# Chunk attention and a routed expert layer: v loaded by pairs of chunks over all 128 partitions, in a ring of eight places

## The chip, the cores and the metric

The kernel runs on one core of a Trainium2 chip. The metric is the device time of one execution, in microseconds (us). Three timed runs of the kernel before gave 680.16, 674.33 and 673.17 us; their median is 674.33 us. One further execution was recorded by the hardware profiler, and all views below come from it.

## The reference

Two blocks follow each other. The first is attention inside chunks of 64 rows: for each of 8 batches and 8 heads, 576 rows of 64 numbers are cut into 9 chunks, and a row sees only its own chunk.

```python
scores = scale * np.matmul(q_c, k_c.transpose(0, 1, 2, 4, 3))
scores = scores - np.max(scores, axis=-1, keepdims=True)
attn = np.exp(scores)
attn = attn / (np.sum(attn, axis=-1, keepdims=True) + 1e-09)
out = np.matmul(attn, v_c)
```

The result becomes 4608 tokens of 512 numbers. The second block sends each token to the one of 8 experts whose embedding is most alike (cosine), computes `relu(x @ w1[e]) @ w2[e]` with w1 of 512 x 1024 and w2 of 1024 x 512, and scales by the probability of that expert. All is float32: q, k and v are 9.4 MB each, w1 and w2 16.8 MB each.

## The kernel before, in words

**Tiles of the attention.** A pair of chunks is 128 rows, so the 72 chunks of all batches make NT = 36 pairs, counted by t. A pair may cross from one batch to the next. For each pair q and k of all 8 heads are loaded as [128 rows, 8 heads, 64] (`load_qk`). `turn_qk` transposes them on TensorE. `scores` makes, for each of 4 head pairs i, each parity of the head (par) and each of the pair's two chunks (c), one 64x64x64 matmul. Its operands lie in rows 64*par and up of SBUF, its result in rows 64*c and up of one of two PSUM banks, the bank of par. VectorE subtracts the maximum, ScalarE takes the exponential (`weights`), TensorE transposes back (`turn_a`), and `values` multiplies with v, which carries a column of ones that gives the row sum. `values` ends with VectorE writing x into `xr`, a ring of NX = 8 places, and GpSimd (POOL) writing the row numbers beside it (the iota of L681).

**v before.** `load_v(b)` (L592 to L601) loads a whole batch: for each head one transfer into 64 partitions (even heads partitions 0 to 63, odd heads 64 to 127), 9 chunks of 256 bytes in each partition. Two buffers `v0` and `v1` alternate by batch. Batch 0 comes in two parts (chunks 0 to 3, then 4 to 8), batch 1 at t = 1, and each later one when pair t nears it; a buffer must have been read to its last chunk before its next batch may be loaded.

**The order of the work.** Everything is recorded in the order in which the code is written (L1037 to L1094): a loop over t from -3 to 38 issues `turn_a(t)`, `turn_qk(t+3)`, `load_qk(t+7)`, `scores(t+2)`, `turn_x(t-1)`, `values(t)`, `weights(t+2)`, and, every fourth pair, the routing (`logits`, `pick`, `place`). Each engine and each DMA queue works through its own list in that order and stops at the first item whose inputs aren't there. Two queues matter. SP's queue holds the first four k tiles, all of v, nine transfers that clear places of the table `spots` (`clear_first`, L567 and L569), then the first expert inputs (`load_early` at t = 26 to 28 and 33) and the first expert weights (`load_first`, w1 at t = 28, w2 at t = 30). GpSimd's queue holds q, the other k tiles, the iota, small constants (one group in each round to t = 16), and `put`: an indirect transfer (L813) that scatters the finished x rows of a pair to `spots` by expert. The x of pair w is put in round w + 6, and its place in `xr` is wanted again by pair w + 8. In the built program a transfer on a queue also waits until the one eight before it has landed.

**The experts.** From `hidden_part` on, groups of 64 tokens for two experts at a time go through w1 (`hidden_fast`, a seven-product scheme, L328) and w2 (`result`, L401), about 37 steps. w1 for the first steps is used from t = 34 on (`early_parts`). `result` ends with ScalarE scaling into a tile `y` of one buffer (L420, L421) and an indirect transfer of it to the output (L428). For this input the last step is an odd one with one group of tokens (`one_group`, 256 columns).

Of the kernel before, what the change touches and what calls it, by code (L numbers as in the profile page):

```python
# [9 lines left out]
FP32 = mybir.dt.float32  # L10
# [8 lines left out]
P = 128  # L19
CH = 64  # L20
# [5 lines left out]
def kernel(  # L26
# [11 lines left out]
    nc = tc.nc  # L38
    B, H, S, Dh = q.shape
    E, D = moe_expert_emb.shape  # L40
    F = moe_w1.shape[2]
    N = B * S
    NPAIR = H // 2
    KD = D // P
# [4 lines left out]
    Q = 32  # L49
# [355 lines left out]
    def result(j, ps_y):  # L405
        d = mo.pop(j)
        ps = ps_y.tile([P, D], FP32, tag="y", name="y_ps")
        one_group = j == LEAST
        w = D // 2 if one_group else D
        for c in range(KF):  # L410
            for r in range(P // Q):
                t0, s, d0 = (r % 2, 0, w * (r // 2)) if one_group else (r, r // 2, 0)
                nc.tensor.matmul(  # L413
                    ps[Q * r : Q * r + Q, 0:w],
                    lhsT=d["hT"][:, c, Q * t0 : Q * t0 + Q],
                    rhs=w2_sb[s][buf_of(j)][:, c, d0 : d0 + w],
                    start=(c == 0),
                    stop=(c == KF - 1),
                )
        y = bp.tile([P, D], FP32, tag="y", name="y", bufs=1)  # L420
        nc.scalar.activation(y[:, 0:w], ps[:, 0:w], AF.Copy, scale=gate_of.pop(j))  # L421
        to, at, bound = out, spot[:, j % SPOTS, TOK : TOK + 1].bitcast(I32), N - 1
        if one_group:

            at2 = bp.tile([P, 1], I32, tag="at2", name="at2")
            nc.vector.tensor_scalar(at2, at, 2.0, second, ALU.mult, ALU.add)
            to, at, bound = out.rearrange("n (s d) -> (n s) d", s=2), at2, 2 * N - 1
        ins = nc.gpsimd.indirect_dma_start(  # L428
            out=to,
            out_offset=bass.IndirectOffsetOnAxis(ap=at, axis=0),  # L430
            in_=y[:, 0:w],
            in_offset=None,
            bounds_check=bound,
            oob_is_err=False,
        )
        tc.declare_no_dep(ins.ins, group="rows", reason="blocks hold different tokens")
        tc.add_to_no_dep_group("rows", ins.ins)
# [8 lines left out]
    with (  # L446
# [7 lines left out]
    ):  # L454

        pad(one, 40, "pad_one")
        v_sb = [one.tile([P, NPAIR, NCB, VW], FP32, name=f"v{i}") for i in range(2)]
        NX = 2 * RB
        xr = one.tile([P, NX, W], FP32, name="xr")
        blank = one.tile([P, W], FP32, name="blank")  # L460
# [108 lines left out]
            nc.sync.dma_start(out=spots[SPARE : SPARE + G, :], in_=blank[0:G])  # L569

        before = one.tile([P, E], BF16, name="before")
        qk_t, qkT, v_t, st = {}, {}, {}, {}

        def load_qk(t):

# [13 lines left out]
                    done += n  # L589
                qk_t[nm, t] = x.rearrange("p h d -> p (h d)")  # L590

        def load_v(b, c0=0, c1=NCB, eng=nc.sync):  # L592

            t = v_sb[b % 2]
            for h in range(H):
                r0 = CH * (h % 2)
                eng.dma_start(
                    out=t[r0 : r0 + CH, h // 2, c0:c1, 0:Dh],
                    in_=v[b, h].rearrange("(c k) d -> k c d", k=CH)[:, c0:c1],
                )  # L600
            v_t[b] = t  # L601

        def turn_qk(t):
            for nm in ("kx", "qx"):
# [11 lines left out]
        def scores(t):  # L616
            qx, kx = qkT.pop(("qx", t)), qkT.pop(("kx", t))
            ps = ps_s.tile([P, 2, 512], FP32, tag="sc", name="sc")
            sc = ps[:, :, 0 : NPAIR * CH].rearrange("p r (i k) -> p r i k", k=CH)
            for i in range(NPAIR):  # L620
                for par in range(2):
                    for c in range(2):
                        r0, c0 = CH * par, CH * c
                        nc.tensor.matmul(
                            sc[CH * c : CH * c + CH, par, i],
                            lhsT=qx[r0 : r0 + CH, i, c0 : c0 + CH],
                            rhs=kx[r0 : r0 + CH, i, c0 : c0 + CH],
                            start=True,
                            stop=True,
                        )  # L630
            mx = wk.tile([P, 2, NPAIR], FP32, tag="mx", name="mx")
            nc.vector.tensor_reduce(mx, sc, axis=AX.X, op=ALU.max)
            a = wk.tile([P, NPAIR, 2, CH], FP32, tag="a", name="a", bufs=3)
            nc.vector.tensor_tensor(
                a.rearrange("p i r k -> p r i k"),
                sc,
                mx.unsqueeze(3).to_broadcast([P, 2, NPAIR, CH]),
                ALU.subtract,
            )
            st[t] = {"a": a}  # L640
# [14 lines left out]
        def values(t):  # L655
            d = st[t]
            ps = ps_v.tile([P, 2, 512], FP32, tag="pv", name="pv")
            pv = ps[:, :, 0 : NPAIR * (Dh + 1)].rearrange("p r (i d) -> p r i d", d=Dh + 1)
            for i in range(NPAIR):
                for par in range(2):  # L660
                    for c in range(2):
                        b, cb = divmod(2 * t + c, NCB)
                        r0 = CH * par
                        nc.tensor.matmul(
                            pv[CH * c : CH * c + CH, par, i],
                            lhsT=d["aT"][r0 : r0 + CH, i, CH * c : CH * c + CH],
                            rhs=v_t[b][r0 : r0 + CH, i, cb, 0 : Dh + 1],
                            start=True,
                            stop=True,
                        )  # L670
            rs = wk.tile([P, 2, NPAIR], FP32, tag="rs", name="rs")
            nc.vector.tensor_scalar(rs, pv[:, :, :, Dh], 1e-9, None, ALU.add)
            nc.vector.reciprocal(rs, rs)
            x = xr[:, t % NX, 0:D]
            nc.vector.tensor_tensor(
                x.rearrange("p (i r d) -> p r i d", r=2, d=Dh),
                pv[:, :, :, 0:Dh],
                rs.unsqueeze(3).to_broadcast([P, 2, NPAIR, Dh]),
                ALU.mult,
            )  # L680
            nc.gpsimd.iota(  # L681
                xr[:, t % NX, D + TOK : D + TOK + 1].bitcast(I32),
                pattern=[[0, 1]],
                base=P * t,
                channel_multiplier=1,
            )
            st[t] = {"x": x}
# [318 lines left out]
        load_qk(1)  # L1006
        for x in v_sb:
            nc.vector.memset(x[:, :, :, Dh : Dh + 1], 1.0)
        load_v(0, 0, 4)
        load_qk(2)  # L1010
        load_qk(3)
        norm_experts()
        nc.gpsimd.memset(xr[:, :, D:W], 0.0)
# [18 lines left out]
                hidden_part(j, s, b, w1_sb, None, None, ps)  # L1032

        early_t = 26
        ends = {sum(sizes[: b + 1]) - 1: b for b in range(len(sizes))}
        constants, clears = constant_parts(), clear_first()
        for t in range(-3, NT + 3):  # L1037

            if 0 <= t < NT:
                turn_a(t)  # L1040
            if t == early_t - 1:
                count_early()
            if t + 3 < NT:
                turn_qk(t + 3)
                if t + 7 < NT:
                    load_qk(t + 7)
            if t == -2:
                load_v(0, 4, NCB)
            if t - 2 in ends:
                logits(ends[t - 2])  # L1050
            if t == NT:
                turn_x(t - 1)
            early_parts(t, 0)
            if 0 <= t + 2 < NT:
                scores(t + 2)
            if t - 2 in ends:
                copy_logits(ends[t - 2])
            if 0 <= t - 1 < NT - 1:
                turn_x(t - 1)
            if t - 3 in ends:  # L1060
                place(ends[t - 3])
            if 0 <= t < NT:
                values(t)
                b = (2 * t + 2) // NCB + 1
                if b not in v_t and b < B and t > 1:
                    load_v(b)
            if t == NT - 8:
                load_first(w1_sb, w1_rows)
            if t == NT - 6:
                load_first([w[0] for w in w2_sb], w2_rows)  # L1070
            if 0 <= t + 2 < NT:
                weights(t + 2)
            if t - 2 in ends:
                pick(ends[t - 2])
            if early_t <= t < early_t + XBUF:
                load_early(t - early_t)

            put(1 if t < NT - 2 else 2)
            if t == NT - 3:
                turn_xb(0)  # L1080
                load_early(XBUF)
            if t == NT - 1:
                turn_xb(1)
            early_parts(t, 1)
            if t == -2:
                turn_experts()
            if t >= 0:
                next(constants, None)
            if t >= 1:
                next(clears, None)  # L1090
                next(clears, None)
            if t == 1:
                load_v(1)
        groups()  # L1094
        pad_places()
        put(len(to_put))
# [148 lines left out]
```

## Time and profile before

| | |
|---|---|
| median of 3 runs | 674.33 us (673.17 to 680.16) |
| profiled execution, its own time | 673.4 us |
| its span (first to last record) | 671.6 us |
| TensorE (PE) busy over the span | 626.3 us, 93% |
| VectorE (DVE), ScalarE (ACT), GpSimd (POOL) busy | 425.9, 427.7 and 175.2 us |
| first and last `values` of the attention | start at 20.80 and 160.91 us |
| q1 (SP's queue): packets, bytes | 82824, 72.84 MB |
| q0 (GpSimd's queue): packets, bytes | 11696, 38.04 MB |
| transfers of v | 72, all from SP, 64 to 144 KB each |

How to read it: a line of the page or of the timeline gives the engine, the line of the kernel (L664 is line 664), the operation, output and inputs, and shape. In the timeline the first two numbers are start and length in us; like instructions in a row are merged, so a merged length covers their overlap. A bracket at the end tells how long the engine had been idle just before, and whose end released it. SPq is the issuing of transfers on SP, not their landing. The DMA row is the mean busy share of the core's 16 DMA engines; overlapping packets can make a share above 1.

### The profile page before, as it was taken

Reading aid. Unit: us, or ns where it says so; the run is one execution under the profiler, and the core shown is the slowest. Engines: PE = TensorE matmul, PEld = TensorE weight load, DVE = VectorE, ACT = ScalarE, POOL = GpSimd, SP = SyncE. Lnnn points to the kernel's source line nnn. Section 1 sums busy time; section 2 is a strip of 40 time slices with the busy share of each in tenths; the row PEclk is TensorE's granted clock in tenths of the full one; section 3 lists DMA queues with packets and bytes.
Section 4 is the critical chain, followed back from the end, with each engine's and each line's share of the span. In section 5 each row is a group of like instructions: output and inputs, shape, how many; then the busy total and the mean of one; then the engine's idle time right before and its main releaser. Section 6 shows DMA issues by size and latency. Waiting matters only on the chain. (4 is left out here: it accounts for less than half of the span.)

```text
span 671.6 us, 24878 instructions
## 1 busy us (share of the span) xinstructions
PE 626.3 (93%) x9744; PEld 343.6 (51%) x9744; DVE 425.9 (63%) x1140; ACT 427.7 (64%) x758; POOL 175.2 (26%) x255
## 2 busy tenths in 40 slices
PE   4988999999899979999999999988999999999993
PEld 3867888786343436555434444433444444444441
DVE  2858888886498535656576566768565667565430
ACT  4656677675225837674867877565877766867740
POOL 6648887843320101002110102202101020100101
PEclk9889899999899979999999999999999999999998
DMA  9898899989818711112787111776821114511101
GB/s 246 221 267 232 245 290 289 278 247 367 316 45 300 294 34 46 44 39 61 286 313 254 54 36 47 283 283 227 325 77 37 50 44 164 175 43 34 50 26 39
DMA packets 94687, 112.67 MB, mean 168 GB/s; under 512 B 52460, under 2 KB 72684, under 8 KB 94552
## 3 DMA queue, kind: packets, MB, share of 16 engines
q1 hardware_dynamic: 82824, 72.84, 34.0%
q0 software_dynamic: 11696, 38.04, 17.1%
q8 instruction: 81, 1.33, 0.8%
q14 instruction: 54, 0.44, 0.2%
q10 hardware_dynamic: 32, 0.02, 0.0%
HBM read 334.71 MB, written 22.69 MB: 532 GB/s over the span
## 5 line engine op out<-in xcount | busy, mean ns | idle before, releaser
L413 PE MATMUL y_ps<-w,hT 128*32 128x512 f32 (+1 forms) x2368 | 265.4, 591 | 3.6 <-DMA w<-in_moe_w_dram 3.6
L361 ACT ACTIVATE h<-C 64x256 f32<-64x256 f32 x264 | 179.0, 678 | 101.8 <-DVE C L374 99.4
L413 PEld LDWEIGHTS y_ps<-w,hT 128*32 128x32 f32 x2368 | 84.1, 111 | 160.0 <-issue 147.6
L428 POOL DMA_INDIRECT out_dram<-y,spot x36 | 35.1, 975 | 414.9 <-ACT y L421 238.7
L374 DVE TENSOR_TENSOR C<-C,h 128x256 f32<-128x256 f32 x231 | 96.1, 416 | 49.8 <-DVEq L299 39.2
L342 PE MATMUL h<-sums,xbT 128*32 128x256 f32 x1056 | 81.0, 380 | 5.0 <-DVEq L299 2.6
L342 PE MATMUL h<-w,S 128*32 128x256 f32 x1056 | 81.4, 379 | 3.2 <-DVE w L291 1.7
L342 PE MATMUL h<-w,xbT 128*32 128x256 f32 x1056 | 68.5, 379 | 0.0
L368 DVE STREAM_TRANSPOSE hT<-h 128x512 f32<-128x512 f32 x66 | 46.7, 708 | 28.2 <-ACT h L361 28.1
L227 DVE TENSOR_SCALAR rn<-rn 128x1 f32<-128x1 f32 x37 | 5.7, 153 | 82.3 <-ACT rn L224 82.3
L342 PEld LDWEIGHTS h<-w,xbT 128*32 128x32 f32 x1056 | 37.7, 110 | 34.1 <-issue 17.0
L342 PEld LDWEIGHTS h<-sums,xbT 128*32 128x32 f32 x1056 | 38.5, 110 | 28.8 <-ACT C L377 4.3
L342 PEld LDWEIGHTS h<-w,S 128*32 128x32 f32 x1056 | 39.1, 110 | 26.0 <-DVE C L374 2.0
L421 ACT ACTIVATE y<-y_ps,gate 128x512 f32<-128x512 f32 (+1 forms) x37 | 25.2, 682 | 37.5 <-issue 25.9
L813 POOL DMA_INDIRECT spots<-xr,dest x36 | 37.4, 1038 | 30.3 <-DVE dest L778 9.8
L203 DVE STREAM_TRANSPOSE xbT<-xin 128x256 f32<-128x256 f32 x73 | 44.5, 649 | 0.5 <-DVE hT L368 0.5
L224 ACT ACT_TABLE_LOAD x34 | 43.6, 1283 | 0.9 <-issue 0.4
L231 ACT ACT_TABLE_LOAD x34 | 43.6, 1283 | 0.6
L342 PE MATMUL h<-sums,S 128*32 128x256 f32 x528 | 40.9, 379 | 0.0
L695 ACT COPY xT<-tr 128x512 f32<-128x512 f32 x36 | 21.1, 585 | 29.9 <-PE tr L693 29.9
L585 POOL DMA_DIRECT2D kx<-in_k_dram x36 | 32.0, 891 | 19.1 <-PE tr L608 18.3
L585 POOL DMA_DIRECT2D qx<-in_q_dram x40 | 34.5, 866 | 0.3 <-PE tr L608 0.2
(202 smaller groups left out, 801.6 us busy)
## 6 DMA issues: line engine op xcount, KB each, us to landing
w<-in_moe_w_dram SPq DMA_DIRECT2D x74, 2048.0 KB
next_w<-in_moe_w_dram SPq DMA_DIRECT2D x67, 2048.0 KB
xin<-spots SPq DMA_DIRECT2D x158, 64.0 KB
qx<-in_q_dram POOLq DMA_DIRECT2D x32, 256.0 KB
v<-in_v_dram SPq DMA_DIRECT2D x56, 144.0 KB
kx<-in_k_dram POOLq DMA_DIRECT2D x28, 256.0 KB
spots<-blank SPq DMA_DIRECT2D x9, 144.0 KB
spot<-spots SPq DMA_DIRECT2D x80, 4.0 KB
```

The source lines that it names most:

```text
L203: nc.vector.transpose(xT[:, :, cols].rearrange("p c (b i) -> p b c i", i=Q), t[:, s * (D // 2) : (s + 1) * (D // 2)].rearrange("p (b i c) ...
L224: nc.scalar.activation(rn, spot[:, j % SPOTS, SQ : SQ + 1], AF.Sqrt)
L231: nc.scalar.activation(sh, sh, AF.Exp, accum_out=gate)
L342: nc.tensor.matmul(ps[t0 : t0 + Q], lhsT=a[:, c, s], rhs=w[:, r], start=c == 0, stop=c == KD // 2 - 1,)
L361: nc.scalar.activation(h[b][G * v : G * v + G, s].rearrange("p (k i) -> p k i", i=Q), x[G * s : G * s + G].rearrange("p (i k) -> p k i", i=Q),
L368: nc.vector.transpose(hT.rearrange("p k (s b i) -> p b s k i", b=2, i=Q)[:, b], h[b].rearrange("p s (k i) -> p s k i", i=Q),)
L374: nc.vector.tensor_tensor(out, a, b, op)
L413: nc.tensor.matmul(ps[Q * r : Q * r + Q, 0:w], lhsT=d["hT"][:, c, Q * t0 : Q * t0 + Q], rhs=w2_sb[s][buf_of(j)][:, c, d0 : d0 + w], start= ...
L421: nc.scalar.activation(y[:, 0:w], ps[:, 0:w], AF.Copy, scale=gate_of.pop(j))
L428: ins = nc.gpsimd.indirect_dma_start(out=to, out_offset=bass.IndirectOffsetOnAxis(ap=at, axis=0), in_=y[:, 0:w], in_offset=None, bounds_ch ...
L585: eng.dma_start(out=x[done : done + n], in_=src[b, :, s : s + n, :].rearrange("h p d -> p h d"),)
L813: ins = nc.gpsimd.indirect_dma_start(out=spots, out_offset=bass.IndirectOffsetOnAxis(ap=at, axis=0), in_=m, in_offset=None, bounds_check=S ...
```

## The change

Three things change.

- v is loaded by windows of two chunks: `load_v(w)` makes one transfer of 128 partitions x 4 heads x 64 for the even heads and one for the odd heads. Even heads hold chunks 2w and 2w+1; odd heads are shifted by a chunk and hold 2w-1 and 2w. At a batch's border a transfer is split in two. The window lies in place w % 8 of a ring of NV = 8.
- So that each operand lies in the right rows, `scores` writes (par, c) to bank `par ^ c`, and `values` takes rows `64 * (par ^ c)` and window t + par*c; the bank of its result stays par.
- Window t + 5 is issued in round t (29 and 30 in round 24, 31 and 32 in round 25), from SP; windows 33 to 36 go through GpSimd's queue in rounds 26 to 29, ahead of `turn_qk` and `load_qk`. Windows 0 and 1 stand between the first k tiles.
- Apart from v, the last odd step writes its result into a tile of the tag `S` and no longer into `y`.

```diff
-        y = bp.tile([P, D], FP32, tag="y", name="y", bufs=1)
+        if one_group:
+            S = late_p.tile([P, 3, KD // 2, 2, Q], FP32, tag="S", name="S", bufs=2)
+            y = S.rearrange("p a c b i -> p (a c b i)")
+        else:
+            y = bp.tile([P, D], FP32, tag="y", name="y", bufs=1)
...
-        v_sb = [one.tile([P, NPAIR, NCB, VW], FP32, name=f"v{i}") for i in range(2)]
+        NV = 8
+        v_sb = [one.tile([P, NV, NPAIR, VW], FP32, name=f"v{i}") for i in range(2)]
...
-        def load_v(b, c0=0, c1=NCB, eng=nc.sync):
-            t = v_sb[b % 2]
-            for h in range(H):
-                r0 = CH * (h % 2)
-                eng.dma_start(
-                    out=t[r0 : r0 + CH, h // 2, c0:c1, 0:Dh],
-                    in_=v[b, h].rearrange("(c k) d -> k c d", k=CH)[:, c0:c1],
-                )
-            v_t[b] = t
+        def load_v(w, eng=nc.sync):
+            for r in range(2):
+                c0, c1 = max(2 * w - r, 0), min(2 * w - r + 2, 2 * NT)
+                while c0 < c1:
+                    b, cb = divmod(c0, NCB)
+                    n = min(c1 - c0, NCB - cb)
+                    p0 = CH * (c0 + r - 2 * w)
+                    eng.dma_start(
+                        out=v_sb[r][p0 : p0 + CH * n, w % NV, :, 0:Dh],
+                        in_=v[b, r::2, CH * cb : CH * (cb + n), :].rearrange("h p d -> p h d"),
+                    )
+                    c0 += n
...
-                            sc[CH * c : CH * c + CH, par, i],
+                            sc[CH * c : CH * c + CH, par ^ c, i],
...
-                        b, cb = divmod(2 * t + c, NCB)
-                        r0 = CH * par
+                        r0 = CH * (par ^ c)
...
-                            rhs=v_t[b][r0 : r0 + CH, i, cb, 0 : Dh + 1],
+                            rhs=v_sb[par][r0 : r0 + CH, (t + par * c) % NV, i, 0 : Dh + 1],
...
-        load_v(0, 0, 4)
+        load_v(0)
         load_qk(2)
+        load_v(1)
         load_qk(3)
...
+        ahead_v = {t: [t + 5] if t < 24 else [] for t in range(-3, NT + 3)}
+        ahead_v[24], ahead_v[25] = [29, 30], [31, 32]
+        for i in range(4):
+            ahead_v[early_t + i] = [33 + i]
...
+            for w in ahead_v[t]:
+                load_v(w, nc.sync if t < early_t else nc.gpsimd)
...
-            if t == -2:
-                load_v(0, 4, NCB)
...
-                b = (2 * t + 2) // NCB + 1
-                if b not in v_t and b < B and t > 1:
-                    load_v(b)
...
-            if t == 1:
-                load_v(1)
```

More of the change, by code (lines that the diff above doesn't have):

```diff
@@ L571 @@
         before = one.tile([P, E], BF16, name="before")
-        qk_t, qkT, v_t, st = {}, {}, {}, {}
+        qk_t, qkT, st = {}, {}, {}
         def load_qk(t):
```

## The prediction

> **What bounds the kernel now.** I began with the page's busy rows and slices.
>
> ```profile
> PE 626.3 (93%) x9744; PEld 343.6 (51%) x9744; DVE 425.9 (63%) x1140; ACT 427.7 (64%) x758; POOL 175.2 (26%) x255
> PE   4988999999899979999999999988999999999993
> DMA  9898899989818711112787111776821114511101
> ```
>
> TensorE is the bound over most of the span. The exceptions are the first slices (16.8 us each) and the end of the attention, where the DMA row is at 8 or 9 and POOL is busy too. The change touches only that first quarter and the last few us, so I then took SP's and TensorE's timelines there.
>
> ```profile
> 1.87 5.62 SPq L597 DMA_DIRECT2D v<-in_v_dram  x8
> 7.54 2.10 SPq L585 DMA_DIRECT2D kx<-in_k_dram  x2
> 9.68 7.49 SPq L597 DMA_DIRECT2D v<-in_v_dram  x8
> 22.36 1.19 SPq L567 DMA_DIRECT2D spots<-blank  x2
> 23.59 9.02 SPq L597 DMA_DIRECT2D v<-in_v_dram  x8
> ```
>
> ```profile
> 14.36 1.09 PE L608 MATMUL tr<-ident,kx 128*128 128x128 f32 x4 [3.89 <-DMA kx<-in_k_dram]
> ...
> 34.13 1.02 PE L664 MATMUL pv<-v,aT 64*64 64x65 f32 x22
> 36.45 0.33 PE L664 MATMUL pv<-v,aT 64*64 64x65 f32 x4 [1.29 <-DMA v<-in_v_dram]
> 37.69 1.07 PE L664 MATMUL pv<-v,aT 64*64 64x65 f32 x6 [0.91 <-DMA v<-in_v_dram]
> 43.63 0.69 PE L664 MATMUL pv<-v,aT 64*64 64x65 f32 x32
> ```
>
> Two holes belong to v. The third k tile stands behind eight v transfers on SP, is issued at 7.54, and TensorE idles 3.89 us for it at 14.36. Batch 1 stands behind the clears, which wait for a GpSimd memset; it is issued from 23.59 to 32.6, and pair 4 needs it at 34.13. From pair 4 to pair 5 takes 43.63 - 34.13 = 9.5 us.
>
> An undisturbed round lasts 3.3 us from one `values` to the next, and 4.1 to 4.4 where routing falls in. Four rounds took 15.2 us at best with q and k loads running (43.63 to 58.82, 76.66 to 91.90), 3.8 us each. The 35 rounds took 160.91 - 20.80 = 140.1; 35 x 3.8 = 133 and the pair 4 hole (9.5 - 4.3 = 5.2) make 138, so about 2 us are left, nearly all between 58.8 and 76.7 (17.8 us for four). There DVE and POOL show why:
>
> ```profile
> 66.02 0.69 DVE L675 TENSOR_TENSOR xr<-pv,rs 128x512 f32<-128x512 f32 x1 [0.90 <-DMA spots<-xr,dest]
> ```
>
> ```profile
> 133.06 1.05 POOL L813 DMA_INDIRECT spots<-xr,dest  x1 [0.18 <-POOL xr L681]
> ...
> 140.03 0.12 POOL L681 IOTA xr<- 128x1 int32 x1 [2.75 <-DMA spots<-xr,dest]
> ```
>
> A place in `xr` is reused eight pairs on, and its put is issued in the second round before that, some 7 us earlier. The put of 133.06 belongs to the place that the iota of 140.03 wants, so it had taken some 6 us to land. That is close to the limit.
>
> The end:
>
> ```profile
> 657.55 0.69 ACT L421 ACTIVATE y<-y_ps,gate 128x512 f32<-128x512 f32 x1 [5.62 <-issue]
> ...
> 661.68 0.47 ACT L421 ACTIVATE y<-y_ps,gate 128x256 f32<-128x256 f32 x1 [3.45 <-DMA out_dram<-y,spot]
> 662.43 0.99 POOL L428 DMA_INDIRECT out_dram<-y,at  x1 [2.95 <-ACTq L1199]
> ```
>
> The last y waits until the y before it has left its only buffer; TensorE's merged line ends at 650.36 + 10.50 = 660.86.
>
> [...] put waits occur while SP sends v (54.8 to 66). [...] Before, each row half kept to its own bank; after, each half writes both. The trace doesn't show such a case.
>
> **The change, part by part.** Durations are of the profiled execution, span 671.6 us.
>
> 1. *First k tiles.* SP now issues two v transfers, not eight, ahead of the third k: at about 0.65 us each (median of the 72) k goes out near 3 us. Ahead of it on SP are 0.70 MB, and GpSimd's q takes an equal share; 2 x 0.96 MB at the 227 GB/s of the first 10 us are there after 8.5 us, so by 9 to 10. TensorE would want it at 14.36 - 3.89 = 10.47. The fourth k stands one window further: 1.47 MB on SP, about 3 MB in all, near 13, wanted at 18.20 - 3.89 = 14.3. I take the whole hole: -3.9; with q slowed a little, at least -2.5.
>
> 2. *Pair 4.* Windows 0 to 7 wait for no reader, so they follow the k tiles at once; window 5, which pair 4 needs, is the twelfth and thirteenth of the first 17 v transfers. SP's 3.0 MB and GpSimd's equal share end near 25 us, window 5 earlier; pair 4 comes at 34.13 - 3.9 = 30.2. The hole goes: -5.2. What is late next is q and k, on half the rate: tile 7 has about 3.1 MB of GpSimd's queue to itself and ahead, lands near 25, and is wanted near 27.5. Loss up to 1.
>
> 3. *Steady rounds.* The transfers are about as many (72, now 80: 36 even and 37 odd windows and seven splits) and have the same runs and bytes, so SP's issue costs nothing while nothing else waits on SP. A round moves q 0.26, k 0.26, v 0.26 and the put 0.29 MB: 1.08 MB in 3.8 us is 284 GB/s. The slices of before reached 304 to 316 (60 to 70, 80 to 90 and 100 to 110 us). v comes evenly instead of 1.15 MB at a time, so the put waits near 60 to 76 should shrink: -1.5. Bounds: -3.5 (all that is above 3.8 a round) to +4 (each of some 20 rounds 0.2 late).
>
> 4. *GpSimd's queue, rounds 26 to 29.* Seven transfers at the 0.9 us of a k or q issue are 6.3 us. A round there has k 0.92, q 0.90, iota 0.16 and put 1.05, 3.0 us; with v 4.8, against 3.8. So GpSimd falls back by about 1 us a round, 3 us by round 28. Behind v stand q and k (wanted four rounds on, covered), and the puts, which have no such cover: those of rounds 27 and 28 land 2 to 3 us later, and VectorE's write to `xr`, then TensorE's transpose, wait. The put of 133.06 was already late for the iota by 2.75, which cost TensorE little, as VectorE came to that `xr` only later. I take +1.5, bounds 0 and +5. SP meanwhile is free of batch 7 (issued until 134) and starts w1 earlier than 146; nothing on TensorE waited for w1 or w2 at 157 to 182, so this is worth nothing.
>
> 5. *`par ^ c`.* Number and order of the matmuls stay, and so do two column tiles in a bank at once. 32 pieces (16 matmuls, two each) take 0.6 us. I take 0: in each column half the two row halves still write different banks. Bounds: -0.05 a block (2 blocks x 36, -3.6) [...].
>
> 6. *End.* y of the last step starts at about 661.0 (the y before it followed its matmuls by 0.14), not 661.68: -0.7.
>
> Sum: -3.9 - 5.2 - 1.5 + 1.5 + 0 - 0.7 = -9.8, a span of 661.8. Its own time was 673.4, 1.8 above the span, so 663.6. The median of the runs lies 0.9 above that time: I say 664.5 us, 1.5% under 674.33.
>
> **Rivals.** *DMA is the true bound, the holes only move.* For it: a DMA row at 9 and 261 GB/s on average from 20 to 130 us. Against: 316 GB/s in a slice, and 98 to 202 from 142 to 148. If half the 9.1 us comes back as waits for q, k or puts: about 670, within 1%.
>
> *Continuous v makes every put late.* From about 7 us of put latency on, each further us is one of VectorE's in that round. With 0.7 us in 28 rounds 19.6 comes back, and the time is 684, slower; it ends above 674.33 from 0.35 us a round. For it: the waits above; against: v is a quarter of the bytes and has no bursts.
>
> *Row halves exclude each other in a PSUM bank.* A 128x256 piece of L342 occupies its column tile for about 215 ns (16 pieces over four tiles in 0.86 us), so a 64-column one takes 54. Four tiles at once give 32 x 54 / 4 = 0.43, under the 0.6 of issue; two at once give 0.86. That is +0.26 in each of 72 blocks, 19 us: 664.5 + 19 = 683, slower. It decides as soon as a block exceeds 0.74 us (9.8 / 72 above 0.6). [...] against: the halves meet in different columns only.
>
> *The change doesn't do what it says*: if kx still lands after 14 us, since windows crowd in beside q, part 1 is lost: 668.
>
> **Numbers.** Forecast 0.62; DMA bound or part 1 lost 0.18 together; late puts 0.11, half of them below the bound for slower; banks 0.09. The likeliest case alone spans 659 to 667.5. For 8 in 10 I go from 658 (the forecast with -3.5 in part 3 and nothing lost in 4 is 661, and some of part 5's gain) to 679, which takes in the half of the late puts and leaves out the banks. About 1% is what a measurement here can tell from no change. Faster than 667.6: 0.62; within 1%: 0.18 + 0.05 = 0.23; slower than 681: 0.15.
>
> **What would show it.** No DMA wait of TensorE at L608 after 10 us and none at `values`; first `values` near 16.9, fifth to sixth about 4.3 apart; blocks of `values` still 0.6 to 0.7; the last `values` near 151; last two ACT writes of y 3.4 apart. Wrong: GpSimd's iotas and VectorE's `xr` waiting for puts in most rounds, or `values` blocks above 0.74.

## The result and the profile after

| | before | after |
|---|---|---|
| median of 7 runs each | 676.84 us (673.17 to 680.16) | 670.36 us (667.25 to 672.22) |
| ratio, 95% interval | | 0.9895 (0.9859 to 0.993) |
| profiled execution: span | 671.6 us | 669.0 us |
| the same kernels again, in a later set of runs: median | 670.80 us (20 runs) | 664.62 us (4 runs) |
| span of those profiles | 667.6 us | 661.6 us |

The change makes the kernel about 1.1% faster; the forecast was 1.5% (664.5 to 674.33). The median of 670.36 is inside the range given (658 to 679), 5.9 us above the forecast. Part of that is common to both kernels: the kernel before had a median 2.5 us higher in these seven runs than in its first three.

The page of the changed kernel, the same rows as before:

```profile
PE 625.3 (93%) x9744; PEld 338.5 (51%) x9744; DVE 425.9 (64%) x1140; ACT 428.5 (64%) x758; POOL 181.1 (27%) x262
...
PE   6999999986899999999999999989999999999993
```

TensorE's first three slices went from 4, 9, 8 to 6, 9, 9. The ninth and tenth slice, from 134 to 167 us, went from 9, 9 to 8, 6. So the gain is where it was looked for, and a loss stands at the end of the attention. SP's timeline in the changed kernel:

```profile
1.87 1.77 SPq L606 DMA_DIRECT2D v<-in_v_dram  x2
3.68 0.62 SPq L591 DMA_DIRECT2D kx<-in_k_dram  x1
4.34 2.27 SPq L606 DMA_DIRECT2D v<-in_v_dram  x2
6.65 1.12 SPq L591 DMA_DIRECT2D kx<-in_k_dram  x1
7.81 13.35 SPq L606 DMA_DIRECT2D v<-in_v_dram  x11
```

The third k tile is issued at 3.68 instead of 7.54. The eleven v transfers after the fourth k tile take 13.35 / 11 = 1.2 us each, not 0.65. TensorE in the same profile:

```profile
10.88 1.11 PE L617 MATMUL tr<-ident,kx 128*128 128x128 f32 x4
...
14.74 1.03 PE L617 MATMUL tr<-ident,kx 128*128 128x128 f32 x4
...
16.65 0.65 PE L672 MATMUL pv<-v,aT 64*64 64x65 f32 x32
...
21.64 0.70 PE L672 MATMUL pv<-v,aT 64*64 64x65 f32 x32 [1.47 <-DMA v<-in_v_dram]
22.27 0.99 PE L659 MATMUL tr<-ident,a 128*128 128x128 f32 x4
23.06 1.06 PE L617 MATMUL tr<-ident,kx 128*128 128x128 f32 x4
...
33.11 0.70 PE L672 MATMUL pv<-v,aT 64*64 64x65 f32 x32
...
37.53 0.69 PE L672 MATMUL pv<-v,aT 64*64 64x65 f32 x32
```

Neither the third k tile (10.88) nor the fourth (14.74) is waited for, so the kx wait of 3.89 us is gone, and so is the hole of pair 4 (37.53 - 33.11 = 4.4 instead of 9.5). A new wait stands at pair 1, 1.47 us for v. What follows it costs more than the wait itself: the transposes of 22.27 and 23.06 take 0.99 and 1.06 us where such groups of four took 0.60 to 0.66 from 15.6 to 20.2 us. TensorE runs a round at half speed: the profile gives a granted clock of 0.61 from 22 to 24 us and of 0.54 from 24 to 26.

The late rounds, all engines, where v goes through GpSimd's queue (L606 on POOL):

```profile
134.29 1.05 POOL L821 DMA_INDIRECT spots<-xr,dest  x1 [0.18 <-POOL xr L689]
135.33 0.68 POOL L606 DMA_DIRECT2D v<-in_v_dram  x1
...
142.60 0.13 POOL L689 IOTA xr<- 128x1 int32 x1 [4.71 <-DMA spots<-xr,dest]
142.63 0.69 DVE L683 TENSOR_TENSOR xr<-pv,rs 128x512 f32<-128x512 f32 x1 [1.30 <-DMA spots<-xr,dest]
...
143.47 0.63 PE L701 MATMUL tr<-ident,xr 128*128 128x128 f32 x4 [2.39 <-DVE xr L683]
```

The iota of 142.60 wants the place whose put was issued at 134.29, 8.3 us before (7.0 us in the kernel before, from 133.06 to 140.03). VectorE needs the same place, and now TensorE waits for VectorE, 2.39 us. And the end:

```profile
655.62 0.69 ACT L425 ACTIVATE y<-y_ps,gate 128x512 f32<-128x512 f32 x1 [5.62 <-issue]
...
659.03 0.47 ACT L425 ACTIVATE S<-y_ps,gate 128x256 f32<-128x256 f32 x1 [2.72 <-PE y_ps L413]
```

The two writes are 3.41 us apart, not 4.13, and the last one waits for TensorE and no longer for the transfer ahead of it.

A table of the starts of `values` and of the last expert step, from TensorE's timelines of both pairs of profiles, puts the difference in its places:

| stretch, us | before | after | difference | before, second | after, second | difference | forecast |
|---|---|---|---|---|---|---|---|
| start of pair 0 | 20.80 | 16.65 | -4.2 | 18.54 | 16.76 | -1.8 | -3.9 |
| pairs 0 to 5 | 22.83 | 20.88 | -2.0 | 23.94 | 20.26 | -3.7 | -5.2 |
| pairs 5 to 28 | 90.84 | 92.07 | +1.2 | 91.14 | 89.52 | -1.6 | -1.5 |
| pairs 28 to 35 | 26.44 | 33.48 | +7.0 | 26.12 | 30.29 | +4.2 | +1.5 |
| pair 35 to the last `result` | 489.45 | 485.35 | -4.1 | 486.51 | 484.08 | -2.4 | 0 |
| from there to the end | 21.24 | 20.57 | -0.7 | 21.35 | 20.69 | -0.7 | -0.7 |
| span | 671.6 | 669.0 | -2.6 | 667.6 | 661.6 | -6.0 | -9.8 |

### The profile page after: what moved, and what is told of

The parts are those of the page before. It is cut to its first block, busy times and chain, and to the rows that moved or that the text cites. A ratio compares the mean times of both kernels' runs of the same rounds, so it can differ in the third digit from the quotient of the medians.

```text
span 669.0 us, 24904 instructions
## 1 busy us (share of the span) xinstructions
PE 625.3 (93%) x9744; PEld 338.5 (51%) x9744; DVE 425.9 (64%) x1140; ACT 428.5 (64%) x758; POOL 181.1 (27%) x262
## 3 DMA queue, kind: packets, MB, share of 16 engines
q8 instruction: 81, 1.33, 0.8%
## 5 line engine op out<-in xcount | busy, mean ns | idle before, releaser
L413 PEld LDWEIGHTS y_ps<-w,hT 128*32 128x32 f32 x2368 | 81.8, 110 | 161.5 <-issue 152.6
L425 ACT ACTIVATE y<-y_ps,gate 128x512 f32<-128x512 f32 x36 | 24.7, 687 | 28.0 <-issue 19.2
L703 ACT COPY xT<-tr 128x512 f32<-128x512 f32 x36 | 21.1, 586 | 33.4 <-PE tr L701 29.5
```

The source lines that it names most:

```text
L413: nc.tensor.matmul(ps[Q * r : Q * r + Q, 0:w], lhsT=d["hT"][:, c, Q * t0 : Q * t0 + Q], rhs=w2_sb[s][buf_of(j)][:, c, d0 : d0 + w], start= ...
```

## The experiments

My theory after the first profile: both holes are closed by the order of SP's queue, and the forecast's missing microseconds are the late rounds, where puts land too late for the eight places of `xr`. Rivals: w1, which SP now loads 12 us earlier (134.03 instead of 146.12), takes the DMA engines from the puts; the layout over 128 partitions, not the order, makes the gain; or TensorE's own half-speed stretches decide. The runs were made in four sets, each on one chip with its own runs of the kernel before, so ratios stand beside each other within a set first of all.

**Both kernels again.** No edit; a second profile of each, taken in the second set.

> The changed kernel unaltered, a second trace of it beside the experiments, on one chip with them. If the length of the first rounds and of rounds 28 to 35 in the first trace is the kernel's (9.98 us from the first to the third values, 33.5 us from pair 28 to 35), it comes back within 1 us. If pauses of TensorE that change from execution to execution made it, one of the two is shorter by 2 us or more.

> The kernel before unaltered, a second trace of it. The two holes at v (3.9 us ahead of the third k tile's transposes, 5 us at pair 4) come back within 0.5 us each, since they are a matter of order on SP. The other rounds may differ by 1 to 3 us over the attention.

The changed kernel: 664.62 us, ratio 0.9883 (0.9834 to 0.9931). The kernel before against itself: 0.9978 (0.9959 to 0.9997), so a ratio within a few thousandths of another tells nothing. The second profile of before has both holes again, though neither within the expected half microsecond: 2.79 us at the third k instead of 3.89, and 10.8 us from pair 4 to pair 5 instead of 9.5:

```profile
35.28 0.33 PE L664 MATMUL pv<-v,aT 64*64 64x65 f32 x4 [1.88 <-DMA v<-in_v_dram]
```

The second profile of the changed kernel has neither that nor the v wait of pair 1. Pairs 0 to 2 take 6.9 us instead of 9.9, and pairs 28 to 35 take 30.3 instead of 33.5; by the expectation some 3 us of each length belonged to the first execution. At pairs 3 to 5 TensorE now stops twice with nothing in the profile's wait list to end it (more on this below):

```profile
26.93 0.69 PE L633 MATMUL sc<-kxT,qxT 64*64 64x64 f32 x30 [0.89 <-issue]
...
32.73 0.56 PE L672 MATMUL pv<-v,aT 64*64 64x65 f32 x20 [0.86 <-issue]
```

The late rounds have the same kind of waits as in the first:

```profile
145.40 0.69 DVE L683 TENSOR_TENSOR xr<-pv,rs 128x512 f32<-128x512 f32 x1 [1.35 <-DMA spots<-xr,dest]
...
149.47 0.69 DVE L683 TENSOR_TENSOR xr<-pv,rs 128x512 f32<-128x512 f32 x1 [1.56 <-DMA spots<-xr,dest]
...
150.30 0.63 PE L701 MATMUL tr<-ident,xr 128*128 128x128 f32 x4 [2.29 <-DVE lmax L745]
```

The wait of 1.56 runs on through VectorE's routing work (lmax) to TensorE, 2.29 us. The stretches of 4 us from there on (length; busy time of TensorE, its weight loads, VectorE, ScalarE and GpSimd with the number of instructions; granted clock, DMA share, GB/s):

```profile
146.00:150.00 4.00, 1.87 (x40) 1.39 (x40) 2.30 (x7) 2.20 (x5) 1.12 (x2) 1.00 0.81 320
150.00:154.00 4.00, 3.42 (x57) 2.34 (x61) 3.73 (x15) 1.21 (x3) 1.48 (x3) 0.69 0.45 151
154.00:158.00 4.00, 3.76 (x72) 2.30 (x68) 0.60 (x3) 1.69 (x4) 3.21 (x5) 0.88 0.93 276
```

TensorE is busy 1.87 of 4 us in the first, and the clock in the next two is 0.69 and 0.88: 4 x 0.31 + 4 x 0.12 = 1.7 us are lost to half speed. In pairs 28 to 35 TensorE idles 4.3 us here and 2.2 us in the second profile of before. So of the 4.2 us of the late rounds some 2.1 are waits and 1.7 their echo. The v wait of pair 1 was a thing of the first execution.

**w1 and w2 later.**

```diff
-            if t == NT - 8:
+            if t == NT - 5:
                 load_first(w1_sb, w1_rows)
-            if t == NT - 6:
+            if t == NT - 4:
```

> The changed kernel with the first w1 issued in round 31 and the first w2 in round 32, not 28 and 30. Theory A (w1, 4 MB on SP from 134 us on, slows the landing of GpSimd's puts while v, q and k stand on the same queue): the time from values of pair 28 to pair 35 falls from 33.5 us to 27 or 28, GpSimd's iota waits for puts fall from 12 us to under 6, and the time falls by 3 to 5 us, unless w1 is then late for the early expert parts. Theory B (the v windows on GpSimd's queue delay the puts by their issue): waits and rounds 28 to 35 stay, time within 1 us.

662.64 us, ratio 0.9857 (0.9813 to 0.99). Pairs 28 to 35 take 30.0 us, as the 30.3 of the changed kernel, and GpSimd's iotas wait for puts just as long in all (10.8 us against 10.0). The early w1 doesn't delay the puts. The ratio isn't told apart from the changed kernel's.

**Windows 33 to 36 from SP (e2_vsp).**

```diff
-                load_v(w, nc.sync if t < early_t else nc.gpsimd)
+                load_v(w)
```

> The changed kernel with windows 33 to 36 issued from SP as all others. Theory B (seven v issues on GpSimd, 5 us, push the puts back): GpSimd's waits for puts and VectorE's at xr go, pairs 28 to 35 take 28 to 30 us in place of 33.5, time 3 to 5 us less. Theory A (w1's bytes slow the puts): w1 goes out some 3 us later behind v, waits shrink by a third at most, time within 2 us.

664.89 us, ratio 0.9884 (0.9843 to 0.9925): no gain. Pairs 28 to 35 shrink from 30.3 to 27.8 us by their starts, so v on GpSimd's queue did cost about 2.5, of which 1.7 are a stretch at half speed that doesn't come here. The expected end of the waits for puts did not come: GpSimd's iotas wait 13.6 us in all (10.0 in the changed kernel) and VectorE's writes 2.7 us from 131 us on. And pair 35 stops halfway. TensorE's timeline of this kernel:

```profile
152.97 0.34 PE L672 MATMUL pv<-v,aT 64*64 64x65 f32 x6
155.67 1.13 PE L672 MATMUL pv<-v,aT 64*64 64x65 f32 x26 [2.37 <-DMA v<-in_v_dram]
```

And SP's:

```profile
142.66 6.48 SPq L153 DMA_DIRECT2D xin<-spots  x2
...
151.68 1.04 SPq L606 DMA_DIRECT2D v<-in_v_dram  x1
```

The last window stands behind the loads of the first expert rows, issued slowly from 142.66 to 151.6, and goes out at 151.68; TensorE waits 2.37 us for it. The forecast had counted what v delays on GpSimd's queue, but not that SP's queue is no better place at that time.

**Window 2 ahead of the fourth k tile (e4_win2).** Against the v wait of pair 1.

```diff
         load_v(1)
+        load_v(2)
         load_qk(3)
```

> The changed kernel with window 2 of v issued ahead of the fourth k tile. Pair 1 waits 1.47 us for window 2, and TensorE's matmuls run at half speed for a round behind that wait. If the wait is the order on SP (mine): no v wait at pair 1, from the first to the third values 7 us in place of 9.9, all later pairs about 3 us earlier, time up to 3 us less. If SP's share of the transfers is what binds (rival): the fourth k tile is then late by 1 to 2 us and nothing is won.

665.75 us, ratio 0.9901 (0.9867 to 0.9936). Pairs 0 to 2 take 7.8 us, as against 9.9 and 6.9 in the two profiles of the changed kernel, and pair 0 starts at 17.99, since the fourth k is late instead:

```profile
16.13 0.63 PE L617 MATMUL tr<-ident,kx 128*128 128x128 f32 x4 [2.62 <-DMA kx<-in_k_dram]
```

In these runs, what was put first in the first 10 us chose who waited.

**The order alone (e5_border).** Before's layout and tiles; only SP's order is changed.

```diff
         load_qk(1)
-        load_v(0, 0, 4)
         load_qk(2)
+        load_v(0, 0, 4)
...
             if t == -2:
                 load_v(0, 4, NCB)
+                load_v(1)
...
-            if t == 1:
-                load_v(1)
```

> The kernel before with v loaded as before, batch by batch into 64 partitions, in a changed order alone: the third k tile ahead of the first eight v transfers, and batch 1 directly behind batch 0, ahead of the transfers that clear places. If the gain is the order on SP's queue (mine): both holes go, first values near 17, pair 4 to 5 near 4.3 us, time 6 to 9 us under before and no worse than the changed kernel. If the gain needs the windows over 128 partitions: the holes move to later pairs, and the time is within 3 us of before.

670.76 us, ratio 0.9967 (0.9943 to 0.999), not told apart from before's 0.9978. Yet both holes are gone but for a wait of 1.34 us at the fourth k: pair 0 starts at 17.92, and pair 5 follows pair 4 by 4.7 us. The time came back at pairs 8 to 12, which take 21.0 us instead of 15.3. SP's timeline shows what batch 1's early load pushed aside:

```profile
25.93 6.13 SPq L567 DMA_DIRECT2D spots<-blank  x6
32.16 9.42 SPq L597 DMA_DIRECT2D v<-in_v_dram  x8
41.63 1.79 SPq L567 DMA_DIRECT2D spots<-blank  x2
43.47 0.60 SPq L569 DMA_DIRECT2D spots<-blank  x1
```

Batch 2 wants the buffer that pair 4 still reads. It stands in SP's queue ahead of the last three clears, and no put may go before the clears. GpSimd's and VectorE's timelines:

```profile
48.02 1.11 POOL L813 DMA_INDIRECT spots<-xr,dest  x1 [5.43 <-DVE qxT L613]
```

```profile
58.30 0.69 DVE L675 TENSOR_TENSOR xr<-pv,rs 128x512 f32<-128x512 f32 x1 [3.29 <-DMA spots<-xr,dest]
```

The first put waits 5.43 us with GpSimd's whole queue behind it. The bracket names VectorE, whose copy had long been done; what it waited for besides is the clears, issued until 44.1, and in the next run, with the clears out earlier, this wait is 1.36 us. So the queue behind a waiting load must be emptied first, which the next run does.

**The order alone, with the clears ahead (f1_border2).** As above, and three clears a round.

```diff
             if t >= 1:
                 next(clears, None)
                 next(clears, None)
+                next(clears, None)
```

> The kernel before with its 64-partition batches of v and its output tiles, and only SyncE's order changed, as in e5_border (third k tile ahead of the first v transfers, batch 1 right behind batch 0), and now three clears of a first-row block a round instead of two, so that all nine stand ahead of batch 2's loads. If the order alone is the gain, and e5_border lost it only because batch 2's loads, which wait for the values of pair 4, stood ahead of the last clears and so of the first put: pairs 8 to 12 take 15.3 to 16.5 us instead of 21.0, no put waits for the clears for more than a microsecond, the last values begin near 152 to 155 us, and the time is within 1% of the changed kernel's (ratio to the kernel before 0.98 to 0.99). If the layout over 128 partitions itself is needed (64-partition batches of about 300 KB come in bursts that delay puts), pairs 8 to 12 or a later batch still take over 18 us and the ratio stays at 0.995 or above.

670.48 us, ratio 0.9916 (0.9889 to 0.9942). Pairs 8 to 12 take 16.5 us, as most steady stretches of four in this set. SP's and GpSimd's timelines show why:

```profile
27.81 7.72 SPq L567 DMA_DIRECT2D spots<-blank  x8
35.58 0.65 SPq L569 DMA_DIRECT2D spots<-blank  x1
36.32 9.81 SPq L597 DMA_DIRECT2D v<-in_v_dram  x8
```

```profile
45.70 1.11 POOL L813 DMA_INDIRECT spots<-xr,dest  x1 [1.36 <-ACT aT L652]
```

The clears are out before batch 2, and the first put waits for no transfer. So two moved lines and a new one give about the gain of the changed kernel in this set (0.9905 for its near copy below); the ring over 128 partitions is one way to get there and wasn't needed for it here. Hole 1 isn't closed here: the fourth k tile now stands behind the eight v transfers, and TensorE waits 3.89 us for it at 17.64. The pair 4 hole is. And the last values begin at 163.3, not at 152 to 155: pairs 28 to 35 take 31.8 us, though no v goes through GpSimd's queue and VectorE waits only 0.4 us for puts in all. TensorE stops for 1.55 us there ("issue", at 149.88) and runs 3.4 us at half speed after it. So late rounds can be lost without the change's seven transfers.

**Twelve places for finished rows (e6_nx12).** v's places shrink to 96 numbers to make room: with 128, what this memory pool holds would take 74.75 KB in each partition, and 69.875 are left.

```diff
-    VW = 2 * Dh
+    VW = 96
...
-        NX = 2 * RB
+        NX = 3 * RB
```

> The changed kernel with twelve places for finished x in place of eight, and v's rows 96 elements apart in place of 128 to make room. If late puts take back what the new order wins: no waits of the iota or of VectorE at xr for a put, pairs 28 to 35 in 26 to 28 us, time 4 to 8 us under the changed kernel on the same chip. If TensorE's pauses do it: waits gone, time within 2 us of it.

659.67 us, ratio 0.9817 (0.9746 to 0.9887), the lowest of all, 5 us under the changed kernel in the same set (the intervals overlap). No engine waits more than 0.2 us for a put from start to end, and pairs 28 to 35 take 26.5 us, as before's 26.1.

**Its control, and a combination (f3_vw96, f2_nx12_vsp).** The same width of 96 with eight places (first line of the diff alone), and twelve places with all of v from SP (with `load_v(w)` as above).

> The changed kernel with the v places 96 instead of 128 numbers wide and eight places for rows, as a control for e6_nx12: if the width does nothing, the ratio to the kernel before is the changed kernel's, 0.985 to 0.99, pairs 28 to 35 take 30 us or more with waits for landed puts; if the width was what e6_nx12 gained, 26.5 us without such waits.

> The changed kernel with twelve instead of eight places for the rows to be put (v places 96 instead of 128 numbers wide to make room, as e6_nx12) and all v transfers from SyncE. If the issues on GpSimd's queue still cost something when no put wait is left: pairs 28 to 35 under 26.5 us and the time 1 to 2 us below e6_nx12's 659.7. If the puts' landing was all that the late rounds had too much, and the issues were hidden: pairs 28 to 35 at 26.5 as in e6_nx12 and the same time within 1 us. A third way: windows 33 to 36 on SyncE wait there for their places, and TensorE waits for v about 2.4 us near pairs 9 and 10 as in e2_vsp: time 661 to 662.

The control: 672.05 us, ratio 0.9933 (0.9898 to 0.9969), iotas waiting 12.1 us for puts and pairs 28 to 35 in 34.6 us. So it is the places, not the width, that end these waits. The combination: 671.33 us, ratio 0.9929 (0.9894 to 0.9964). It has no put wait and no v wait in the late rounds, and yet pairs 28 to 35 take 32.9 us: all three expectations failed. TensorE's timeline there:

```profile
143.69 0.34 PE L633 MATMUL sc<-kxT,qxT 64*64 64x64 f32 x6
144.28 0.34 PE L633 MATMUL sc<-kxT,qxT 64*64 64x64 f32 x5 [0.24 <-issue]
...
145.73 0.52 PE L633 MATMUL sc<-kxT,qxT 64*64 64x64 f32 x16 [0.39 <-issue]
147.05 1.09 PE L701 MATMUL tr<-ident,xr 128*128 128x128 f32 x4 [0.79 <-DVE xr L683]
148.07 1.15 PE L672 MATMUL pv<-v,aT 64*64 64x65 f32 x32
```

One block of 32 score matmuls, 0.69 us elsewhere, is issued in batches of five with pauses of some 0.4 us ("issue": nothing that the profile shows was waited for) and lasts 2.57. After it everything runs at half speed (values 1.15 instead of 0.70) until 153. Here the loss comes with no wait for a transfer at all.

**The end undone.** The changed kernel with its y tile as before.

```diff
-        if one_group:
-            S = late_p.tile([P, 3, KD // 2, 2, Q], FP32, tag="S", name="S", bufs=2)
-            y = S.rearrange("p a c b i -> p (a c b i)")
-        else:
-            y = bp.tile([P, D], FP32, tag="y", name="y", bufs=1)
+        y = bp.tile([P, D], FP32, tag="y", name="y", bufs=1)
```

> The changed kernel with its output tiles as before (one place again, no S tile for the small groups). By the forecast's part 6 the last two writes of y are 4.1 us apart instead of 3.4, and the time is 0.7 us longer than the changed kernel's, which is less than the times tell apart; only the trace can show it. If the other experts' steps also gained by the freed place, the end is more than 1 us later from the last values on; if the place did nothing, the two writes stay 3.4 apart.

671.10 us, ratio 0.9905 (0.9879 to 0.9932). The wait is back:

```profile
654.99 0.69 ACT L421 ACTIVATE y<-y_ps,gate 128x512 f32<-128x512 f32 x1 [5.62 <-issue]
...
659.03 0.47 ACT L421 ACTIVATE y<-y_ps,gate 128x256 f32<-128x256 f32 x1 [3.35 <-DMA out_dram<-y,spot]
```

4.04 us apart against 3.41: the S tile is worth 0.6 us.

**Order and twelve places together (g1_border2_nx12).** f1_border2's order with NX = 3 * RB and VW = 96, in a set of its own.

> The kernel before with f1_border2's order of SyncE (third k tile ahead of the first v transfers, batch 1 behind batch 0, three clears a round) and twelve places for the rows to be put (v places 96 numbers wide to make room); neither the layout of v over 128 partitions nor v on GpSimd's queue is in it. If what the changed kernel gained is the order, and what it lost in the late rounds is v on GpSimd's queue together with puts that land later than eight places allow: no wait for a landed put is left, pairs 28 to 35 take 26.5 us where four steady pairs take 15.3 (28.5 where they take 16.4), and the ratio to the kernel before is 0.98 or below, as e6_nx12's. If the layout over 128 partitions is what spares the puts, batch loads of 64 partitions cost a steady stretch 1 us or more and the ratio stays at 0.99. If TensorE's half-speed stretches decide more than both, they follow some other idle time and the ratio lies between 0.983 and 0.99 with nothing of it in the waits.

676.48 us, ratio 1.0002 (0.9978 to 1.0026): no gain at all. As expected, no put wait is left; as not expected, pairs 28 to 35 take 33.4 us. Two score blocks, at 137.0 and 149.9, are stretched to 2.18 and 2.74 us as above (last line below). And the pair 4 hole is back in part: pair 5 follows pair 4 by 7.6 us, with a stop of TensorE's own and a wait for v:

```profile
33.78 0.51 PE L664 MATMUL pv<-v,aT 64*64 64x65 f32 x18 [1.78 <-issue]
35.13 0.33 PE L664 MATMUL pv<-v,aT 64*64 64x65 f32 x2 [0.85 <-DMA v<-in_v_dram]
...
152.01 0.61 PE L624 MATMUL sc<-kxT,qxT 64*64 64x64 f32 x24 [0.44 <-issue]
```

So twelve places take the put waits away in all three kernels that have them, but only one of the three kept the time; and the gain of the order alone, seen in f1_border2's set, isn't seen again here. It isn't shown that e6_nx12 is the better kernel on every chip.

## Why the prediction was right, and where it was not

The mechanism held: the two holes were v's, the order of SP's queue makes them, and without them the changed kernel is about 1% faster. That the total came within 6 us of the forecast is in part luck: the holes gave less and the late rounds took more than forecast, and 2.4 to 4.1 us came from a place that the forecast didn't have. No row-half conflict came, the rival with the largest loss: 30 of the 36 `values` blocks of the changed kernel's first profile and 34 of its second took 0.64 to 0.71 us (33 and 35 in the kernel before), and the mean of one of the matmuls is 225 ns before and 227 after. The longer ones aren't row halves: f1_border2 and g1_border2_nx12, with the layout of before, have 11 and 9 of them. No trace had shown such a conflict when I gave it a price, and none shows it now. By its terms:

1. *First k tiles*, -3.9: -4.2 and -1.8 in the two pairs of profiles. In the second the kernel before had waited 2.8 us only, and the changed one still waited 0.4 at the fourth k. The control with places of 96 waited 1.43 and 3.09 us for the third and fourth k with the same order and started pair 0 at 20.19. So the sign is right and the size is that of the luckier case; the wait can move to the fourth k tile.
2. *Pair 4*, -5.2: -2.0 and -3.7. The hole is gone; what was late next wasn't q or k, as I had put it. In the first execution it was v for pair 1 (1.47 us, and a round at half speed after it); why only there isn't shown, since e2_vsp issues the same transfers at the same pace (13.34 us for eleven) and doesn't wait. In the second it was TensorE itself, with the two stops of 0.89 and 0.86 us shown above. Terms 1 and 2 had counted equal shares of SP's and GpSimd's queue. That was my assumption, shown by no view ahead of the result. In the first 10 us of the kernel before the two took 44.3% and 41.0% of the DMA engines' time and moved 0.99 and 1.27 MB. From 7.8 to 21.2 us of the changed kernel's first profile the shares of the time were equal, but not the bytes (packets, MB, share of the 16 engines' time):

```profile
q0 software_dynamic: 774, 2.45, 57.5%
q1 hardware_dynamic: 6491, 1.61, 57.0%
```

   SP's packets are of 248 bytes on average and GpSimd's of 3.2 KB, so SP moved 40% of the bytes.
3. *Steady rounds*, -1.5: -1.6 in the second pair. In the first it was +1.2, but there the changed kernel's four pairs took 16.3 to 16.5 us in most stretches, as those of every kernel of the third and fourth set of experiments, whatever its layout; in the first two sets they took about 15.3. This goes with the set and not with the change: `values` of pair 12 lasts 1.09 to 1.13 us in the changed kernel's first profile and in all five of the last two sets, and 0.70 in the other eight.
4. *GpSimd's queue in the late rounds*, +1.5: this is the term that was mis-sized. It measured +4.2 and +7.0. The working "about 1 us a round, 3 us by round 28" was near, the seven issues being 0.77 us each and not 0.9. It shows in the issue of the puts: in rounds 27 and 28 it comes 3.3 and 4.7 us after the first matmul of `values` in both profiles of the changed kernel, and 1.9 and 1.8 us after it in both of the kernel before and in e2_vsp. Once issued, they took no longer in the second pair of profiles: 4.0 to 7.6 us before and 5.6 to 7.6 after, from the issue to the release of whoever waited. What failed was "cost TensorE little". From 126 to 170 us GpSimd's iotas wait about as long in all before and after (11.0 and 12.0 us in the first pair), but VectorE's writes wait 0.6 us before and 3.0 and 3.6 after: it had almost no slack behind GpSimd. From VectorE the waits run on to TensorE (2.39 and 2.50 us in the first profile, 2.29 in the second), and the last of them in each profile is followed by half speed on TensorE (1.7 us more). By TensorE's idle time and clock, the +7.0 of the first pair are 3.9 of waits, 1.7 of half speed and 1.4 of stretched blocks, and the last aren't the change's. Nor is all of the loss v on GpSimd's queue: with v from SP the second set's rounds 28 to 35 still take 27.8 us, 1.7 more than before's 26.1, and VectorE still waits 2.7 us for puts there. The w1 loads, worth nothing by the forecast, were indeed worth nothing.
5. *`par ^ c`*, 0: right.
6. *End*, -0.7: right, -0.7 in both pairs and 0.6 by the run without it.

A term was missing, and it was a gain in both pairs: from pair 35 to the last `result` the changed kernel is 2.4 to 4.1 us shorter. In the kernel before TensorE waits in expert step 4 for weights, `[3.60 <-DMA w<-in_moe_w_dram]` in its first profile and the first line below in its second; in the changed kernel's second profile the same step waits for VectorE:

```profile
237.93 1.27 PE L413 MATMUL y_ps<-w,hT 128*32 128x512 f32 x4 [4.03 <-DMA w<-in_moe_w_dram]
```

```profile
233.52 7.83 PE L413 MATMUL y_ps<-w,hT 128*32 128x512 f32 x62 [1.91 <-DVE gate L234]
```

I took this for a matter of arrival: a TensorE that reaches this place late waits less there. In the first pair that fits: SP starts loading the rows of the next group at 189.36 before and at 189.46 after, so the 2.2 us that the changed kernel was late at pair 35 were forgiven. In the second it doesn't, since SP starts at 186.35 and 182.32 and the changed kernel is the earlier one. Nor is the wait the change's: e2_vsp and e4_win2, both with the change, wait 2.92 and 3.85 us for weights at this step, and f1_border2, without it, 0.5. So this gain isn't shown to belong to the change.

TensorE's stops with the bracket "issue" are of two kinds, and one goes with transfers that these traces show. Queue q8 carries 81 instruction transfers of 16 KB (`q8 instruction: 81, 1.33, 0.8%` on the page of either kernel). TensorE has some 19,800 recorded instructions, so there is one transfer to about 245 of them. Counted in these instructions, 35 stops, among them all of more than 1 us after the first 15 us of a profile, stand 192 or 193 past a multiple of 256. TensorE passed the first 26 such places 364 times in the fourteen profiles, and never earlier than 2.2 us after the transfer with the same number began (2.23 us at the least in the first profile of the kernel before, 2.44 in that of the changed one). The 35 stops, of 0.17 to 1.78 us, ended 2.2 to 2.9 us after it. That TensorE waits there for the next part of its own program is my reading of place and time; no wait in the profile names it. The two stops in the changed kernel's second profile are of this kind, and so are the 1.55 us of f1_border2 and the 1.78 us of g1_border2_nx12. Ten of the twelve profiles of kernels other than before have such stops at pairs 3 to 5, 0.5 to 2.2 us in all in each; the two of the kernel before have none there. So with the hole closed these stops come in its place, which the forecast's term 2 lacked.

What stays open is the other kind, above all the blocks issued in batches of four or five matmuls, with which the third and fourth set lost so much. These stops don't stand at such places and don't end at a fixed time after a transfer. The blocks do stand at the same matmuls of the program in two kernels (2692 to 2697 and 2930 to 2943, counted from the start, in f2_nx12_vsp and g1_border2_nx12). Nothing in these traces names their cause.

## What to carry to other kernels

List what stands behind each load that has to wait for a buffer, on its queue, and who waits for that: closing a hole by an earlier load moved it to the first put until the clears were put ahead too. Before a transfer is moved to another queue near a hand-over, look at the stretch of both queues there; here each of the two made someone wait 2.4 us. Where a ring's places come free only just in time in the kernel before, a delay that looks covered can be paid in full. And when a hole is closed, ask what the engine reaches next: here, in ten of twelve profiles, it was stops of its own, 0.5 to 2.2 us in all at pairs 3 to 5.

## What the hardware showed

- TensorE fell to half speed (a granted clock of 0.50 from 155.55 to 158.96 us of the changed kernel's first profile) after short waits. Most such stretches last 3.41 us (1.7 us lost), some 6.83 (from 13.78 and from 239.06 in the first profile of the kernel before, from 146.53 in f2_nx12_vsp). In the 3.41 us ahead of such a stretch TensorE had still been busy for 1.8 us (pair 1, after a wait of 1.47 us) and for about 1 (after one of 2.29 us). Not every wait was followed by one: none followed the 2.39 us at 143.47.
- At the places 192 or 193 past a multiple of 256 of its recorded instructions TensorE stopped for up to 1.78 us, and in these traces it never passed one of the first 26 earlier than 2.2 us after the q8 transfer of 16 KB with the same number began.
- TensorE's matmuls were issued in batches of a few with 0.4 us between them while the records show a clock of 1.00: in score blocks (2.57 us in f2_nx12_vsp and 2.74 in g1_border2_nx12, instead of 0.69) and in one expert step, where y_ps took 10.87 us in the changed kernel's first profile, instead of 7.05 for a like step. The same step is long in all five profiles of the last two sets.
- From the issue of a put of 128 rows to the release of whoever waited for it, the late rounds took 4.0 to 7.6 us in both profiles of the kernel before, and 5.6 to 8.3 in both of the changed kernel.
- From 7.8 to 21.2 us of the changed kernel's first profile two busy queues had equal shares of the DMA engines' time (57.0% and 57.5%, the mean share 1.15 with overlapping packets) and unequal bytes (1.61 and 2.45 MB), the smaller packets (248 bytes on average against 3.2 KB) moving less.
- Four steady rounds without a put wait took mostly 15.1 to 15.6 us in the first two sets of experiments and mostly 16.3 to 16.5 in the last two, whatever the kernel, with the same mean times of matmuls and of VectorE's and ScalarE's instructions. What makes the difference isn't shown.
